# Four interleaved attention layers: side tiles in pieces of four matmuls, and an earlier first score in the full layers

## The chip, the cores and the metric

The kernel runs on one core of a Trainium2 chip. The metric is the device time of one execution in microseconds (us); the number given is a median of several runs. A profile is one execution, recorded by the hardware profiler.

## What is computed

Four layers in a row on x of 2048 positions by 512 features, 32 heads of 16: sliding attention (A), full attention (B), A, B. Each layer adds its output to x.

```python
def _A_ref(x, wqkv, wo):            # _B_ref is the same without the mask
    B, S, D = x.shape
    H = 32; Dh = D // H; W = 256
    q, k, v = ...                   # from x @ wqkv, split by heads
    scores = jnp.einsum("bhqd,bhkd->bhqk", q, k) * (Dh ** -0.5)
    idx = jnp.arange(S)
    mask = (idx[:, None] - idx[None, :] >= 0) & (idx[:, None] - idx[None, :] < W)
    scores = jnp.where(mask[None, None], scores, -1e9)
    p = _softmax(scores, axis=-1)
    o = jnp.einsum("bhqk,bhkd->bhqd", p, v)
    return o.transpose(...).reshape(B, S, D) @ wo

x = x + _A_ref(_layernorm(x), A_wqkv, A_wo)
x = x + _B_ref(_layernorm(x), B_wqkv, B_wo)
x = x + _A_ref(_layernorm(x), A_wqkv, A_wo)
x = x + _B_ref(_layernorm(x), B_wqkv, B_wo)
```

## The kernel before

**Attention.** Positions go in 4 chunks of 512 (c), heads in 8 groups of four (qd). Scores are computed transposed, keys by queries, two heads at a time in the two 64-row halves of the array, and ACT takes their exp straight from PSUM (`exps`, L718; exps are L735). In a sliding layer (0 and 2) a group has three units, each with two exps, selects on POOL that zero the masked triangles (L802, L805), and the product with the values (L812), which PE does two units later. Score matmuls are L731. A layer has 4 x 8 x 3 = 96 units. In a full layer (1 and 3) a group has 16 units, one per 128 keys; scores are L727, products with the values L779; a layer has 512 units. PSUM holds two score tiles, so the scores of a pair wait until the exp of the pair before last is done.

**The shift.** Instead of a row maximum, a bound from the squared lengths of queries and keys is subtracted. It comes in as extra rows of the score product: the queries' bound is row 3 of `qs`, the keys' is row 7 of `kf`. For it the squares of all keys are summed by heads on PE (`squares`, L535), reduced on DVE to `km` (L562), over all chunks to `kx` (L600) and made a row `mk` (L602), which goes to `kf` in DRAM (L604); then `kt`, the keys of one group, is loaded (L752). In a full layer no score can run before the last chunk of keys is in.

**Side work.** Everything else is side work, written as generators: keys, queries and values (`project`, `values`), output product with the next layer's norm (`wo`). Its matmuls are made in `mms` (L390): a tile is 12 matmuls, three terms by four blocks, of 128x128 by 512 columns, 0.222 us each by the planner's clock. In the sliding layers and the handoffs a tile is recorded at once (L402). In the full layers a matmul is cut into eight parts of 64x32 (L399), and `yield us` lets the planner put single steps between the scores; `PH["busy"]` says that a tile is open, and `Side.one` (L897) then goes on with it.

`Side` (L883) spreads the side work: after each unit of attention, `step` in a sliding layer runs work until what is spent has caught up with the work due by then:

```python
s0, due = self.spent, self.cost * self.k / (self.steps - 2)
while self.q and self.spent < due and self.spent - s0 < 3:
    c = self.one()
    if c is None or c < 0 and self.spent - s0 >= 2 and due - self.spent < 4:
        break
```

**Handoffs.** Behind a sliding layer's last unit come the works in `tails` (L1188), then the keys' shift, then `lasts` (L1190), then the full layer. `late` marks works that fill the time of the last chunk's norm. PE and SP (which issues the DMAs) run in the order of recording.

Of the kernel before, what the change touches and what calls it, by code (L numbers as in the profile page):

```python
# [19 lines left out]
P = 128  # L20
# [12 lines left out]
HEAD_START = 100  # L33
EB, XB, XNB, WB, VB, OB = 6, 4, 4, 2, 3, 5
# [155 lines left out]
def fast_path(ctx, tc, flag, a_x, a_wqkv, a_wo, b_wqkv, b_wo, out):  # L190
# [199 lines left out]
    def mms(ps, pairs, after=1.6, us=MM):  # L390


        PH["busy"] = PH["full"]
        for i, (a, b) in enumerate(pairs):
# [9 lines left out]
            if i < len(pairs) - 1:  # L404
                if PH["full"]:
                    yield us
            else:
                PH["free"] = clock[0] + (2.0 if PH["full"] else after)
                PH["busy"] = False
    TERMS = ((0, 0), (0, 1), (1, 0))  # L410
# [67 lines left out]
    def project(l, s, c, act, ht=None):  # L478
# [3 lines left out]
        w = weights(ty, s, n, *((0, D, 0) if ht is None else (ht * P, (ht + 1) * P, not act)))  # L482
# [9 lines left out]
        for t in range(NHT) if ht is None else (ht,):  # L492
# [39 lines left out]
            yield -MM if PH["full"] else -12 * MM  # L532
# [20 lines left out]
    def keys(l, c, act, ht=None):  # L553
        sqs = yield from project(l, 1, c, act, ht)

        def rest():
# [4 lines left out]
            with tc.high_priority(HEAD_START):  # L561
                nc.vector.tensor_reduce(KM[l][r, c:c + 1], ph[r], axis=AX.XY if PH["full"] else AX.X, op=ALU.max)  # L562
        pend.append((clock[0] + (4.6 if PH["full"] else 3.6), rest))
# [31 lines left out]
    def key_shift(l, ht=None):  # L595

        settle()
# [3 lines left out]
        m = vp.tile([P, QC], F16, name=f"mk{l}_{ht}", tag="m", bufs=1)  # L601
        nc.vector.tensor_scalar(m[r], ones[r], kx[r], -0.515, op0=ALU.mult, op1=ALU.mult)  # L602
        for t in range(NHT) if ht is None else (ht,):
            nc.sync.dma_start(rows(kf)[8 * t:8 * t + 8, 7, :].rearrange("h (c n) -> h c n", n=QC),  # L604
                              m[32 * t:32 * t + 8, None, :].broadcast_to([8, NQ, QC]))

    def values(l, c, act, halves=(0, 1), tiles=range(4)):
# [18 lines left out]
        for i in tiles:  # L626
# [13 lines left out]
            yield -us if PH["full"] else -12 * us  # L640

    def wo(l, c, tail):
# [4 lines left out]
        for i in range(4):  # L647
# [11 lines left out]
            yield -MM if PH["full"] else -12 * MM  # L659
# [84 lines left out]
    def load_full(l, c, qd):  # L744
        n = f"{l}_{c}_{qd}"
        pair = slice(2 * qd, 2 * qd + 2)
        qt = pp.tile([P, 2, QC], F16, name=f"qt{n}", tag="qt", bufs=2)
        nc.sync.dma_start(qt, qs[1, c][pair].rearrange("r p n -> p r n"))
        kts = []
        for v in range(2):  # L750
# [69 lines left out]
    class Work:  # L820
# [34 lines left out]
        proj = property(lambda self: self.name is not None and self.name[0] in ("K", "Q", "K3", "Q3"))  # L855
# [27 lines left out]
    class Side:  # L883
# [13 lines left out]
        def one(self, force=False):  # L897

            drain()
            if PH["full"] and PH["busy"]:  # L900
# [85 lines left out]
    def attention(l, works):  # L986
# [5 lines left out]
        for t in range(NHT if l == 3 else 1):  # L992
            for c in range(NQ):
                qds = range(2 * t, 2 * t + 2) if l == 3 else range(NQD)
                if l == 1:

                    sd = sd or Side(NT * NQD // 2, works[0], works[1], 0.33)
                    while ("Q", 1, c) not in DONE:
                        sd.one(True)
# [4 lines left out]
                for qd in qds:  # L1004
                    if (l, c, qd) == (1, 0, NQD // 2):
                        sd.finish()
                        sd = Side(NT * NQD * NQ - NT * NQD // 2, works[1], works[2], 0.33)
                    nxt = load(l, c, qd + 1) if qd + 1 in qds else None
                    a = acc[qd % 2 if win else 0]
                    began, u = clock[0], 0  # L1010
                    for f in (attn_win if win else attn_full)(l, c, qd, *ops, a):
# [15 lines left out]
                        elif u:  # L1027
                            sd.step()
# [212 lines left out]
```

## Time and profile before

| | |
|---|---|
| median of 3 runs | 2760.06 us (2759.93 to 2761.41) |
| profiled execution | 2759.5 us, of it span 2757.7 us |
| busy over the span | PE 2496.1 us (91%), ACT 2362.9 (86%), DVE 1094.9, POOL 515.8 |
| chain of work that ended last | ACT 56%, PE 23%, issue 11%, DVE 5%, DMA 3% |

Rows of the profile name an engine, a line, what is written and read, and how often; PEld is the load of weights into the array, SPq a DMA issue on SP. A wait is put down to whoever ended it. A timeline row gives start, length, and in brackets the idle time ahead and its releaser; a run of like instructions is one row (x12). The ends of matmuls are modelled.

### The profile page before, as it was taken

The numbers are of one execution on the slowest core, as the hardware profiler recorded it, in microseconds if no ns is written. First come the engines' busy times: TensorE is split into PE (matmuls) and PEld (weight loads), VectorE is DVE, ScalarE is ACT, GpSimd is POOL, SyncE is SP. The second block draws the span as 40 slices with busy tenths as digits, with TensorE's granted clock in tenths as the row PEclk, the third lists the DMA queues.
The fourth block names the chain that finished last, engine by engine and source line by source line (L and its number), as shares of the span: only waits on it lengthen the run. The fifth ranks groups of instructions, "written<-read, shape, count | busy, mean of one in ns | idle before, by whom it ended". The sixth has DMA issues, their size and how long they took to land.

```text
span 2757.7 us, 112292 instructions
## 1 busy us (share of the span) xinstructions
PE 2496.1 (91%) x50513; PEld 1100.3 (40%) x50513; DVE 1094.9 (40%) x2314; ACT 2362.9 (86%) x2683; POOL 515.8 (19%) x1074
## 2 busy tenths in 40 slices
PE   7888989999989999999998898899899999998987
PEld 3233334444433344444443333534444444433332
DVE  5564554122343335325326566323333333333333
ACT  4556654899999999999995667399999999999997
POOL 1445552001000000100105678100000000000000
PEclk9999999999999999999999999999999999999999
DMA  8888856322342224324225565623232333333332
GB/s 286 226 241 240 244 178 191 96 83 82 100 120 79 86 93 137 102 78 126 93 73 169 157 181 143 175 72 109 84 107 90 98 97 104 112 104 123 114 120 103
DMA packets 335035, 359.67 MB, mean 130 GB/s; under 512 B 113616, under 2 KB 250320, under 8 KB 328144
## 3 DMA queue, kind: packets, MB, share of 16 engines
q1 hardware_dynamic: 334544, 352.40, 42.3%
q8 instruction: 397, 6.50, 1.0%
q14 instruction: 94, 0.77, 0.1%
HBM read 239.60 MB, written 96.99 MB: 122 GB/s over the span
## 4 chain that ended last, share of the span: by engine, by line
ACT 56%; PE 23%; issue 11%; DVE 5%; DMA 3%; POOL 2%; SPq 0%; ACTq 0%; DVEq 0%; POOLq 0%
ACT e L735 55%; PE b L402 10%; PE acc L812 3%; PE acc L779 3%; PE bs L402 2%; PE s L731 2%; PE s L727 2%; PE b L399 1%; POOL e L802 1%; POOL e L805 1%; DMA qt<-qs 1%; DMA kt<-kw 0%; DMA wr<-in_A_wo_dram 0%; DVE ot L694 0%; DMA w<-wd 0%
## 5 line engine op out<-in xcount | busy, mean ns | idle before, releaser
L735 ACT ACTIVATE e<-s 128x1024 f32<-128x1024 f32 (+2 forms) x2432 | 2238.8, 1058 | 121.0 <-PE s L731 95.3
L779 PE MATMUL acc<-e,vt 64*17 64x512 f32 x16384 | 1085.0, 590 | 1.3 <-issue 1.3
L727 PE MATMUL s<-qt,kt 64*32 64x512 f16 x16384 | 849.0, 380 | 130.4 <-ACT e L735 106.6
L727 PEld LDWEIGHTS <-kt 64*32 64x32 f16 x16384 | 406.7, 89 | 944.2 <-issue 868.8
L779 PEld LDWEIGHTS acc<-e,vt 64*17 64x17 f32 x16384 | 280.5, 92 | 61.1 <-issue 1.5
L805 POOL TENSOR_SCALAR_AFFINE_SELECT e<-e 128x256 f32<-128x256 f32 x512 | 224.9, 446 | 196.5 <-ACT e L735 195.4
L802 POOL TENSOR_SCALAR_AFFINE_SELECT e<-e 128x256 f32<-128x256 f32 x448 | 198.1, 449 | 114.1 <-ACT e L735 112.3
L712 POOL TENSOR_TENSOR oh<-o,oh 128x512 f16<-128x512 f32 x31 | 36.1, 1165 | 938.1 <-DVE oh L711 884.8
L812 PE MATMUL acc<-e,vt 128*17 128x384 f32 (+2 forms) x2816 | 204.7, 396 | 5.3 <-POOL e L802 4.0
L731 PE MATMUL s<-qt,kt 64*128 64x384 f16 (+2 forms) x1408 | 129.0, 280 | 64.0 <-ACT e L735 38.2
L415 DVE TENSOR_SCALAR sa<-acc 128x512 f32<-128x512 f32 x64 | 44.3, 692 | 335.4 <-PE acc L779 335.4
L402 PE MATMUL b<-xc,w 128*128 128x512 f16 x696 | 166.1, 390 | 7.0 <-DMA w<-wd 5.8
L677 DVE SCALAR_TENSOR_TENSOR x<-b,x 128x512 f32<-128x512 f32 x122 | 83.9, 688 | 193.0 <-PE b L399 189.8
L402 PEld LDWEIGHTS <-w 128*128 128x128 f16 x816 | 77.4, 100 | 122.8 <-issue 35.8
L521 POOL TENSOR_TENSOR sq<-sp 128x512 bf16<-128x512 f16 x28 | 41.0, 1463 | 442.2 <-DVE sp L515 427.6
L506 ACT ACTIVATE sp<-b 128x512 f16<-128x512 f32 x58 | 34.7, 598 | 103.3 <-PE b L402 91.2
L731 PEld LDWEIGHTS <-kt 64*128 64x128 f16 x1408 | 54.4, 94 | 167.6 <-issue 137.0
L521 POOL TENSOR_TENSOR sq_h<-sp_h 128x512 bf16<-128x512 f16 x27 | 40.1, 1484 | 409.8 <-DVE sp_h L515 409.8
L399 PE MATMUL b<-wo,oh 64*32 64x512 f16 x2592 | 109.9, 376 | 6.2 <-DVE x L677 3.1
L399 PE MATMUL b<-xc,w 64*32 64x512 f16 x2688 | 110.9, 376 | 3.0 <-DVE j L416 2.3
L399 PE MATMUL b<-xc,w_h 64*32 64x512 f16 x2592 | 104.4, 376 | 4.1 <-DVE km L562 3.9
L415 DVE TENSOR_SCALAR j_h<-b 128x512 f32<-128x512 f32 x27 | 18.7, 691 | 218.7 <-PE b L399 187.6
(136 smaller groups left out, 1874.8 us busy)
## 6 DMA issues: line engine op xcount, KB each, us to landing
kt<-kf SPq DMA_DIRECT2D x128, 512.0 KB
qt<-qs SPq DMA_DIRECT2D x128, 256.0 KB
xd<-x SPq DMA_DIRECT2D x96, 256.0 KB
x<-xd SPq DMA_DIRECT2D x96, 256.0 KB
w<-wd SPq DMA_DIRECT2D x22, 1024.0 KB
kt<-kw SPq DMA_DIRECT2D x64, 256.0 KB
qs<-sp SPq DMA_DIRECT2D x48, 256.0 KB
wo<-wd SPq DMA_DIRECT2D x12, 1024.0 KB
```

Source lines behind the costliest of these rows:

```text
L399: nc.tensor.matmul(ps[g:g + 32, r], a[k, g:g + 32], b[k], start=(i == 0), stop=(i == len(pairs) - 1), skip_group_check=True)
L402: nc.tensor.matmul(ps, a, b, start=(i == 0), stop=(i == len(pairs) - 1))
L415: nc.vector.tensor_scalar(dst, ps[0], scale, None, op0=ALU.mult)
L521: nc.gpsimd.tensor_tensor(sq, sp[:, 0], sp[:, 0], ALU.mult)
L677: nc.vector.scalar_tensor_tensor(xs[i], p, 1 / WS, xs[i], op0=ALU.mult, op1=ALU.add)
L727: nc.tensor.matmul(ps[g:g + 32, h], kt[R * h:R * h + R, pr, kc + g:kc + g + 32], qt[R * h:R * h + R, pr], start=True, stop=True, skip_grou ...
L731: nc.tensor.matmul(ps[:, h, s0:s0 + wd_], kt[R * h:R * h + R, pr, kc:kc + P], qt[R * h:R * h + R, pr, qc:qc + wd_], start=True, stop=True)
L735: nc.scalar.activation(e[:, :, w0:w1], ps[:, :, w0:w1], AF.Exp, scale=SCALE)
L779: nc.tensor.matmul(acc[r][32 * h:32 * h + DH + 1, :], V[l, qd // 4, j // 8][k, j % 8, 4 * (qd % 4) + h, :], es_[h // 2][k, h % 2, :], star ...
L802: nc.gpsimd.affine_select(v, v, pattern=[[0, 2], [-1, P]], compare_op=ALU.is_gt, fill=0.0, base=0, channel_multiplier=1)
L805: nc.gpsimd.affine_select(v, v, pattern=[[0, 2], [1, P]], compare_op=ALU.is_ge, fill=0.0, base=0, channel_multiplier=-1)
L812: nc.tensor.matmul(a[32 * h:32 * h + DH + 1, q * P:(q + nb) * P], V[l, (4 * c + j) // 4][:, j % 4, 4 * qd + h, :], es_[h // 2][:, h % 2, s ...
```

## The change

**Pieces of four.** In a sliding layer `mms` now yields after every fourth matmul, so a tile can lie over up to three units; `PH["busy"]` is set there too, and `one` finishes the open tile before it picks other work. **First scores.** The keys of layer 1's last chunk are made in four quarters of the heads (`K1`), as layer 3's already were; only two quarters (layer 1) or one (layer 3) stand ahead of the full layer, the others are side work of it. `early_keys` and `early_queries` load the first half of the first group's keys and its queries at the end of the sliding layer; `key_shift` then writes the row for them straight into that tile in SBUF. The last chunk's values are made ahead of the full layer only for the lower heads and two of four key blocks; the rest (`last_lower`, `upper`) and layer 1's queries of chunk 1 are side work of the full layer. **Queries.** Layer 3's first queries (`Q3(0, 0)`) move from the handoff into layer 2's last chunk.

```diff
+PIECE = 4
     def mms(ps, pairs, after=1.6, us=MM):
-        PH["busy"] = PH["full"]
+        PH["busy"] = PH["full"] or PH["win"]
...
                 if PH["full"]:
                     yield us
+                elif PH["win"] and i % PIECE == PIECE - 1:
+                    yield PIECE * us
...
+    def last(us):
+        return -(1 if PH["full"] else PIECE if PH["win"] else 12) * us
...
-            yield -MM if PH["full"] else -12 * MM
+            yield last(MM)
...
-    def keys(l, c, act, ht=None):
+    def keys(l, c, act, ht=None, then=None):
...
                 nc.vector.tensor_reduce(KM[l][r, c:c + 1], ph[r], axis=AX.XY if PH["full"] else AX.X, op=ALU.max)
+                if then is not None:
+                    then(l, ht)
...
-    def key_shift(l, ht=None):
-        settle()
+    def key_shift(l, ht):
...
+        if ht == 0:
+            for pr in range(2):
+                nc.sync.dma_start(PRE["k"][7:P:R, pr, :].rearrange("r (c n) -> r c n", n=QC),
+                                  m[2 * pr:2 * pr + 2, None, :].broadcast_to([2, 2, QC]))
+        nc.sync.dma_start(rows(kf)[8 * ht:8 * ht + 8, 7, :].rearrange("h (c n) -> h c n", n=QC),
+                          m[32 * ht:32 * ht + 8, None, :].broadcast_to([8, NQ, QC]))
+        DONE["S", l, ht] = clock[0]
+    PRE = {}
+    def early_keys(l):
+        PRE["k"] = pp.tile([P, 2, S // 2], F16, name=f"kt{l}_0_0_0", tag="kt", bufs=3)
+        nc.sync.dma_start(PRE["k"], kf[0:2, :, :S // 2].rearrange("r p n -> p r n"))
+    def early_queries(l):
+        PRE["q"] = pp.tile([P, 2, QC], F16, name=f"qt{l}_0_0", tag="qt", bufs=2)
+        nc.sync.dma_start(PRE["q"], qs[1, 0][0:2].rearrange("r p n -> p r n"))
...
     def one(self, force=False):
-            if PH["full"] and PH["busy"]:
+            if PH["busy"]:
                 return self.piece(PH["last"])
...
+                    while (l, c, qd % 2) == (1, 0, 1) and qd + 1 in qds and ("S", 1, (qd + 1) // 2) not in DONE:
+                        if ("K1", (qd + 1) // 2) in DONE and not PH["busy"]:
+                            settle()
+                        else:
+                            sd.one(True)
...
+                        while not win and (c, qd, u) == (0, 0, NT - 5) and ("V", l, 3, (0,), 2) not in DONE:
+                            sd.one(True)
...
+    def K1(ht, act=False):
+        return Work(later(keys, 1, NQ - 1, act, ht, key_shift), PK / 4, ("K1", ht), [("T", 1, NQ - 1), ("P", 1, 1)], True)
...
-        return [OO(2, 2), T(3, 2), K3(2, 0, True)]
+        return [OO(2, 2), T(3, 2), Q3(0, 0, True), K3(2, 0, True)]
...
+    def last_lower(l):
+        return VV(l, 3, False, (0,), (), range(2, 4))
...
-        a += [Q(1, c, False) for c in (2, 3)]
+        a += [Q(1, c, False) for c in (1, 2, 3)]
...
-        a = [Q3(c + 1, t)] if c < 3 else []
+        a = [last_lower(3)] if (t, c) == (0, 0) else []
+        a += [Q3(c + 1, t)] if c < 3 else []
...
-    works = [[side0(c) for c in range(NQ)], [[upper(1, c) for c in range(3)], side1()], [side2(c) for c in range(NQ)],
+    works = [[side0(c) for c in range(NQ)], [[last_lower(1), K1(2), upper(1, 2), upper(1, 3), K1(3)], side1()], [side2(c) for c in range(NQ)],
...
-    tails = {0: [VV(1, 2, True, (0,)), OO(0, 3, True), VV(1, 1, True, (0,), late(1)), Q(1, 1, True, late(1)), T(1, 3), K(1, 3)],
-             2: [VV(3, 0, True, (0,)), OO(2, 3, True), VV(3, 1, True, (0,), late(3)), VV(3, 2, True, (0,), late(3)), Q3(0, 0, True, late(3)), T(3, 3), K3(3, 0, True)]}
-    lasts = {0: [VV(1, 3)], 2: [VV(3, 3, True, (0,)), VV(3, 0, True, (1,))]}
+    tails = {0: [VV(1, 2, True, (0,)), OO(0, 3, True), VV(1, 1, True, (0, 1), late(1)), VV(1, 0, True, (1,), late(1)), T(1, 3), K1(0, True), K1(1, True)],
+             2: [VV(3, 0, True, (0,)), OO(2, 3, True), VV(3, 1, True, (0,), late(3)), VV(3, 2, True, (0,), late(3)), VV(3, 0, True, (1,), late(3)), T(3, 3), K3(3, 0, True)]}
+    lasts = {l: [VV(l + 1, 3, True, (0,), (), range(2))] for l in (0, 2)}
...
             attention(l, works[l] + [tails[l]])
+            settle()
+            early_keys(l + 1)
+            early_queries(l + 1)
             all_of(tails[l], lasts[l])
-            key_shift(l + 1, 0 if l else None)
             all_of(lasts[l], works[l + 1][0])
+            settle()
```

The order of the instructions shows it at three places. First PE in layer 2, chunk 1, between the groups qd 1 and qd 2 (`s_` are scores, `acc` the products with the values, `oh` and `wo` the operands of an output tile). Before, PE goes from the products of one unit straight to the next scores:

```order
L812 MATMUL acc_82<-e_1_1_0_0_29748,vt_0_0_0_15544 17x128 x2
L812 MATMUL acc_82<-e_1_1_0_1_29758,vt_0_0_0_15544 17x128 x2
L812 MATMUL acc_82<-e_1_1_0_0_29748,vt_1_0_0_21586 17x384 x2
L812 MATMUL acc_82<-e_1_1_0_1_29758,vt_1_0_0_21586 17x384 x2
L731 LDWEIGHTS kt_1_2_29738
L731 MATMUL s_1_2_0_0_29858<-qt_1_2_29739,kt_1_2_29738 128x128
```

In the change four matmuls of an output tile stand there; these are the last of them and the scores behind:

```order
L403 LDWEIGHTS oh_0_5_29808
L403 MATMUL b_30186<-wo_0_30049,oh_0_5_29808 128x512
L760 LDWEIGHTS kt_1_2_30103
L760 MATMUL s_1_2_0_0_30228<-qt_1_2_30104,kt_1_2_30103 128x128
L760 LDWEIGHTS kt_1_2_30103
```

and the same tile (b_30186) goes on behind the products of the next unit:

```order
L842 MATMUL acc_82<-e_1_1_1_0_30145,vt_1_0_0_22380 17x256 x2
L842 MATMUL acc_82<-e_1_1_1_1_30154,vt_1_0_0_22380 17x256 x2
L403 LDWEIGHTS oh_0_5_29808
L403 MATMUL b_30186<-wo_0_30049,oh_0_5_29808 128x512
L403 LDWEIGHTS oh_0_7_30046
L403 MATMUL b_30186<-wo_0_30049,oh_0_7_30046 128x512
```

So the tile was cut after its eighth matmul, and a unit that had no side work has four matmuls of it. Second, PE ahead of layer 1, behind the last key tile (`sq` the squares of a quarter of the heads, `wv` the value weights). Before, the square sums of all four quarters are followed by four value tiles of 512 columns, then by the first scores:

```order
L546 MATMUL b_5637<-sq_1_3_2_5613,hsum 32x512
L546 LDWEIGHTS hsum
L546 MATMUL b_5637<-sq_1_3_3_5633,hsum 32x512
L402 LDWEIGHTS xc_3_5384
L402 MATMUL bs_5655<-wv_3_0_0_5544,xc_3_5384 128x512
```

In the change the first quarter's square sum follows two key tiles, and a value tile has 256 columns:

```order
L403 LDWEIGHTS w_1_3_h_5530
L403 MATMUL b_5554<-xc_3_5388,w_1_3_h_5530 128x512
L553 LDWEIGHTS hsum
L553 MATMUL bs_5567<-sq_1_3_h_0_5548,hsum 32x512
L403 LDWEIGHTS xc_3_5388
L403 MATMUL b_5586<-wv_3_0_0_5552,xc_3_5388 128x256
```

Two such value tiles, with the second quarter's square sum between them, remain ahead of the first scores. Third, SP at the same place, before:

```order
L526 DMA kf<-sp_1_3_3_5630 128x2x512
L527 DMA kf<-sp_1_3_3_5630 128x512
L604 DMA kf<-mk_None 8x4x512 x4
L752 DMA kt_0_0_0_5724<-kf 128x2x1024
L752 DMA kt_0_0_1_5726<-kf 128x2x1024
```

and in the change, where kt's first half (kt_0_0_0) was loaded long before and only its row comes now, behind a weight load and the key writes:

```order
L371 DMA wv_3_0_2_5584<-wd_2_111 128x8x256
L533 DMA kf<-sp_1_3_h_1_5577 128x2x512
L534 DMA kf<-sp_1_3_h_1_5577 128x512
L616 DMA kt_0_0_0_5232<-mk_0_5572 2x2x512 x2
L618 DMA kf<-mk_0_5572 8x4x512
```

The write of mk to DRAM and the load of kt behind it no longer stand between the last keys and the first scores; a small copy within SBUF does.

36 lines of the change are left out of this document (20 added, 16 removed).

## The prediction

> **What bounds the kernel now.** First the page's slices: which engine is full, and where.
>
> ```profile
> PE   7888989999989999999998898899899999998987
> ACT  4556654899999999999995667399999999999997
> ```
>
> Each digit is a 69 us slice. ACT stands at 9 in two long stretches, the full layers 1 and 3, and at 4 to 6 in the sliding layers, where PE is at 8 or 9 but not full. I cut the span at these borders. The columns are the stretch and its length, then the busy time of PE, weight loads, DVE, ACT and POOL with their counts, PE's granted clock, DMA's busy share, GB/s.
>
> ```profile
> 54.00:437.00 383.00, 339.37 (x2950) 135.34 (x2949) 201.62 (x476) 233.31 (x308) 195.23 (x483) 0.94 0.79 226
> 437.00:495.00 58.00, 55.71 (x328) 28.65 (x328) 24.37 (x55) 17.60 (x35) 1.96 (x6) 1.00 0.69 207
> 495.00:1446.00 951.00, 887.39 (x22560) 400.61 (x22552) 320.24 (x640) 943.32 (x1026) 59.46 (x46) 1.00 0.31 94
> 1446.00:1732.00 286.00, 253.86 (x2574) 99.06 (x2562) 175.22 (x406) 190.57 (x228) 198.91 (x483) 0.99 0.55 160
> 1732.00:1783.00 51.00, 45.31 (x327) 30.85 (x319) 20.58 (x49) 12.61 (x28) 0.00 (x0) 0.97 0.72 204
> 1783.00:2740.00 957.00, 871.34 (x21614) 386.24 (x21622) 307.86 (x577) 943.97 (x1024) 57.52 (x42) 1.00 0.33 103
> ```
>
> In order: sliding layer 0, a handoff, full layer 1, sliding layer 2, a handoff, full layer 3. In a full layer ACT works 943 us of 951 and of 957: its exps set the time, and a full layer can only start earlier or lose. The handoffs are PE work in a row with ACT nearly idle. In the sliding layers nothing is full, so I ask what PE waits for in layer 2 and in layer 0 (us in total, times, longest).
>
> ```profile
> PE s L731 <- ACT e L735: 23.5, 43, 1.1
> ...
> PEld acc L812 <- POOL e L802: 9.0, 26, 1.2
> ```
> ```profile
> PEld L731 <- DMA kt<-kw: 15.0, 3, 7.9
> PE s L731 <- ACT e L735: 14.8, 22, 1.6
> ```
>
> Layer 2 loses 23.5 + 9.0 = 32.5 us in many small waits for exps and selects, which an even spread of the side work can remove. Layer 0 loses 15.0 in three long waits for kt, with DMA 0.79 busy, and only 14.8 in small ones for ACT.
>
> **Part 1, pieces of four.** PE's timeline in layer 2:
>
> ```profile
> 1611.83 0.61 PE L731 MATMUL s<-qt,kt 64*128 64x384 f16 x8
> 1612.37 1.06 PE L812 MATMUL acc<-e,vt 128*17 128x128 f32 x16
> 1613.36 2.76 PE L402 MATMUL b<-wo,oh 128*128 128x512 f16 x12
> 1616.06 0.61 PE L731 MATMUL s<-qt,kt 64*128 64x128 f16 x8
> 1616.60 1.06 PE L812 MATMUL acc<-e,vt 128*17 128x256 f32 x16
> 1617.64 0.40 PE L731 MATMUL s<-qt,kt 64*128 64x256 f16 x4
> 1618.56 0.39 PE L731 MATMUL s<-qt,kt 64*128 64x256 f16 x4 [0.52 <-ACT e L735]
> ```
>
> A unit with a tile takes 4.23 us (1611.83 to 1616.06), a plain one 1.58 (1616.06 to 1617.64), and behind a plain one the next scores wait 0.52 for ACT. ACT was idle beside the tile and is late beside the plain unit. Counted along PE's order, layer 2 has before its last unit 62 plain units, 32 with a tile and one with two; the change has 26 plain, 41 with four matmuls, 20 with eight, 5 with twelve, 3 with sixteen. If waits go with the plain units, 32.5 us become 32.5 x 26/62 = 13.6, a gain of 19. Against it: one tile more (the last layer's first queries, 12 matmuls, 2.6 us), and 69 - 33 = 36 more units in which PE enters side work. An entry costs 0.11 us, as the chain of waits shows: a tile behind attention takes 2.70, one behind another tile 2.59.
>
> ```profile
> 447.04 2.59 PE b L402 x12
> ```
> ```profile
> 1609.20 2.70 PE b L402 x12
> ```
>
> That is 4 us, so 19 - 2.6 - 4 = 12 gained. A unit with four matmuls would take 1.58 + 4 x 2.59/12 + 0.11 = 2.55; ACT's work is 190.57/96 = 2.0 per unit and POOL's 198.91/96 = 2.1, so it should not wait, but only 0.5 us covers it, and selects come in lumps. I take **-10** for layer 2, near the 12 that the counts give, between -26 (all waits go) and +6.6 (none goes).
>
> [...]
>
> In layer 0 the side work is the same 792 matmuls of 512 columns; plain units go from 30 to 18. Of 14.8 us of ACT waits 14.8 x 12/30 = 6 could go, 1 returns as entries, and where DMA is the limit the rest turns into longer waits for kt. In the order nearly all side jobs end at the same unit or one later, so K and Q are not written sooner. I take **-3**, between -12 and +8.
>
> **Part 2, first handoff.** PE's timeline before, from the moment the last chunk's normalized x lands:
>
> ```profile
> 471.79 2.75 PE L402 MATMUL bs<-xc,w 128*128 128x512 f16 x12 [1.14 <-DMA xc<-xh]
> 474.47 0.40 PE L546 MATMUL b<-sq,hsum 128*32 128x512 bf16 x4
> ...
> 484.40 2.76 PE L402 MATMUL bs<-wv,xc 128*128 128x512 f16 x12
> ...
> 494.86 0.62 PE L727 MATMUL s<-qt,kt 64*32 64x512 f16 x16
> ```
>
> Behind 471.8 stand four key tiles and four value tiles to 494.86. The change leaves two key tiles and two half value tiles there. Ahead of 471.8 the work is equal (a query chunk of four tiles out, four tiles of values in), so I keep that start: xc lands by DMA, not by PE. Two key tiles end at 477.1. The first one's square sum follows at once, then km, kx, mk on DVE:
>
> ```profile
> 484.50 0.69 DVE L562 TENSOR_REDUCE km<-b 128x1 f32<-128x512 f32 x1 [0.40 <-PE b L546]
> ...
> 485.50 0.35 DVE L602 TENSOR_SCALAR mk_None<-ones,kx_None 128x512 f16<-128x512 f16 x1
> ```
>
> From 484.50 to 485.85 is 1.35 us; with the square sum's 0.4 ahead of it mk stands at about 478.9. On SP the two writes of the second key tile are ahead of its copies into kt. The second handoff has rows for both steps: its key tile ends at 1770.0 (Part 3) and its second write goes out at 1771.90 and is issued by 1772.35, 2.4 us behind; and a small copy of mk at 1774.93 lets the load that waits for it go at 1777.53, 2.6 us later.
>
> ```profile
> 1771.90 0.45 SPq L527 DMA_DIRECT2D kf<-sp_h  x1
> ...
> 1774.93 0.32 SPq L604 DMA_DIRECT2D kf<-mk  x1
> ...
> 1777.53 1.41 SPq L752 DMA_DIRECT2D kt<-kf  x3
> ```
>
> So the copies go at 477.1 + 2.4 = 479.5 and 479.8, and the first scores run near 482.4. The half value tiles must not come later: their weights can go only when the first key tile is done, at 474.4, and take less than a load twice their size, so they land by 479.6, and 2 x 1.3 us more are 482.2.
>
> ```profile
> 454.84 5.22 DMA w<-wd
> ```
>
> I take **-12.5** (494.86 to 482.4), between -16 (the scores follow the key tiles' own work) and -6 (half).
>
> **Part 3, second handoff.**
>
> ```profile
> 1758.69 2.76 PE L402 MATMUL bs<-xc,w_h 128*128 128x512 f16 x12 [0.19 <-DMA w_h<-wd]
> ...
> 1765.56 4.45 PE L402 MATMUL bs<-xc,w_h 128*128 128x512 f16 x12 [3.79 <-DMA x<-xd]
> ...
> 1771.35 0.38 PE L546 MATMUL bs<-sq_h,hsum 128*32 128x512 bf16 x1 [1.03 <-ACT sq_h L519]
> ...
> 1783.07 0.63 PE L727 MATMUL s<-qt,kt 64*32 64x512 f16 x16 [0.75 <-DMA kt<-kf]
> ```
>
> The query tile at 1758.69 moves into layer 2, half of the value tiles from behind the key tile come ahead of it and cover most of the wait to 1765.56. The key tile then takes 2.7 instead of 4.45 if the clock holds: in the trace it ran at 0.50 just there.
>
> ```profile
> 1766.20:1769.60 3.40, 3.40 (x9) 1.21 (x8) 0.00 (x0) 0.00 (x0) 0.00 (x0) 0.50 0.64 211
> ```
>
> From its end at 1768.2: 1.4 to the square sum (1770.0 to 1771.35), 0.4 for it, 1.35 on DVE, 0.3 for the first copy, 2.6 for the second to land: first scores near 1774.3, **-9**, between -11 and -4. [...]
>
> **Part 4, full layers.** Layer 1 takes 50 matmuls of 512 columns more while it runs and 10 behind its last scores. At 2.59/12 = 0.216 each (a whole matmul's time, which its eight parts share here), the 10 are 2.2 us; the 50 are 11 us of PE under 951 - 887 = 64 us of slack, but in the later chunks they raise the densest stretches, and PE has little room in those:
>
> ```profile
> 1350.00:1400.00 50.00, 48.46 (x1240) 22.29 (x1225) 17.62 (x34) 49.88 (x55) 5.61 (x4) 1.00 0.28 90
> ```
>
> I take **+5**, from +2 to +13. Layer 3 takes 12 more: **+0.5**, from 0 to 3. What is late next behind the early scores is kt's second half, read back from DRAM behind the row's write: 2.6 us for the write and 1783.07 - 1777.53 = 5.5 for the load, 8 us, while the first half feeds 8 units of 951/512 = 1.86, 15 us.
>
> **Sum.** -3 - 12.5 + 5 - 10 - 9 + 0.5 = -29 against the profiled execution's 2759.5 us (span 2757.7 and 1.8 around it) gives 2730.5. The median of the three runs is 2760.06, 0.6 more: **2731**.
>
> **Rivals.** (a) *Pieces give nothing*: PE's waits move to exps and to kt, entries stay. Layer 2 +6.6, layer 0 +1: -12.5 - 9 + 5 + 0.5 + 7.6 = -8.4, 2751.7. For it: ACT and POOL work 2.0 and 2.1 us per unit, so units of 2.55 us run three engines near their limit. Against: ACT's idle beside every tile is plain in the rows. (b) *Handoffs give half*, since SP, in order, holds the row copies behind a weight load and the key writes, or x lands later: -11 for -21.5, 2741. (c) *Pieces give all*: layer 2 -26, layer 0 -12: 2706. (d) *Slower*: the tiles end later in pieces, so the K and Q writes come later, and the chunks' first loads, which wait for them, stall PE. In layer 0 one such wait was 7.9 us. If each of the six later chunk starts of layers 0 and 2 had one such wait more, that is 6 x 7.9 = 47 us: 2778. It decides once a chunk's queries end within a landing of its start; in the order they end 10 units or more ahead, and that speaks against it. (e) *It does not do what it says*: the early loads wait for their buffers, scores start as before; then only Part 1 and the smaller PE work remain, near (b).
>
> **Chances.** Forecast 0.62 (2718 to 2740), (b) with (e) 0.13, (a) 0.13, (c) 0.07, (d) 0.05. The range 2715 to 2750 leaves out (d), (c) and the upper half of (a). A change of 0.2%, 5.5 us, is about what a measurement of this kernel can tell from none. Faster by more: 0.62 + 0.13 + 0.07 + most of (a) = 0.91; within: 0.04; slower: 0.05.
>
> **What would show it.** Right: layer 2's PE waits for ACT near 10 instead of 23.5 us, four-matmul units near 2.55 us; first full scores 12.5 and 9 us sooner after the sliding layers' ends; the second handoff's key tile at full clock; ACT still over 0.98 in the full layers. Wrong: plain 0.5 us waits now in the units with four matmuls (a), a long wait for mk or wv ahead of the first scores (b), long kt waits at chunk starts (d), ACT below 935 of 951 us in layer 1 (Part 4).

## The result, and the profile after

The changed kernel takes **2725.1 us** (median of four runs, 2721.88 to 2731.55) beside 2760.4 us for the kernel before, measured with it (four runs, 2759.93 to 2761.41): the ratio is 0.9876, with a 95% interval of 0.9862 to 0.9890. It is faster by 35 us, six more than forecast and inside the range. The profiled execution took 2721.88 us, 2720.2 of it span.

The stages below are cut at PE's rows: a sliding layer from its first score to the end of its last product with the values, a handoff from there to the first full score, a full layer from its first score to the next layer's first (layer 3: to the end of its last score). In line numbers of the changed kernel, L760 are the sliding scores, L764 the exps, L842 the products, L756 the full scores, L403 a side tile, L553 a square sum, L832 and L835 the selects.

| us | layer 0 | handoff 1 | layer 1 | layer 2 | handoff 2 | layer 3 |
|---|---|---|---|---|---|---|
| before | 385.6 | 55.8 | 953.2 | 284.2 | 50.8 | 953.6 |
| after | 374.4 | 45.6 | 954.4 | 274.8 | 42.6 | 953.5 |
| moved | -11.2 | -10.2 | +1.2 | -9.4 | -8.2 | -0.1 |
| forecast | -3 | -12.5 | +5 | -10 | -9 | +0.5 |

Each cell is one profile, and the moves add to 37.9 us, as the profiled execution is the fastest of the four. In the other profiles below, layer 0 with pieces took 372.0 to 377.7 us, layer 1 of the change 952.7 to 955.2 and layer 2 of the change 274.1 to 276.6, so that a move of one or two us in a cell says nothing.

First the slices of the page, in tenths of a slice's time:

```profile
PE   7888999999998999999998999899999999988997
ACT  4575664999999999999995777499999999999996
```

The picture is that of before: ACT is full in the full layers, and PE is near full but not full in the sliding ones. What moved is idle time of PE, some of its busy time in layer 0, and the PE work of the handoffs. The windows of the two sliding layers and the two handoffs (length, then busy time of PE, weight loads, DVE, ACT, POOL, then PE's granted clock, DMA share, GB/s), of before for the sliding layers:

```profile
53.49:439.04 385.55, 341.85 (x2968) 136.15 (x2969) 201.88 (x476) 233.31 (x308) 196.86 (x487) 0.94 0.79 226
1448.06:1732.25 284.19, 252.05 (x2551) 98.74 (x2547) 175.22 (x406) 189.55 (x226) 198.91 (x483) 0.99 0.55 160
```

and of the changed kernel:

```profile
53.67:428.04 374.37, 337.60 (x2969) 133.46 (x2969) 201.90 (x476) 237.05 (x308) 197.66 (x487) 0.96 0.81 234
1428.04:1702.80 274.76, 251.99 (x2569) 95.49 (x2561) 175.23 (x408) 193.39 (x228) 201.12 (x483) 0.98 0.62 175
428.04:473.68 45.64, 41.84 (x244) 23.93 (x242) 20.40 (x50) 11.73 (x26) 0.32 (x1) 0.96 0.55 156
1702.80:1745.47 42.67, 37.65 (x279) 26.60 (x278) 19.19 (x47) 10.59 (x24) 0.00 (x0) 1.00 0.70 189
```

In layer 2 PE's busy time is the same (252.05 and 251.99), though a tile came in: the whole gain is idle time, 284.19 - 252.05 = 32.1 us before and 22.8 after. In layer 0 the idle time fell from 43.7 to 36.8 us, and PE's busy time by 4.3 us at a clock of 0.96 instead of 0.94.

What PE and the weight load (PEld) waited for in layer 2 of the changed kernel (us in total, times, longest):

```profile
PE s L760 <- ACT e L764: 11.8, 20, 1.1
PE s L760 <- DMA qt<-qs: 7.4, 3, 3.6
...
PEld acc L842 <- POOL e L832: 9.9, 34, 1.3
```

The waits for exps are half of the 23.5 us of before. Before, all of them stood behind a unit without side work; now 10.7 of the 11.8 us do. The weight load's waits for selects, 9.0 us before, did not fall. But the weight load waited while PE still worked on earlier matmuls: PE's own waits for selects, 0.5 and 0.2 us in two rows before and 0.6 now, were small from the start. The first of these rows:

```profile
PE acc L812 <- POOL e L802: 0.5, 1, 0.5
```

Layer 0 of the changed kernel:

```profile
PE s L760 <- ACT e L764: 8.6, 14, 1.9
PE b L403 <- DVE km L569: 5.5, 1, 5.5
```
```profile
PEld L760 <- DMA kt<-kw: 10.4, 3, 8.7
```

Here too the waits for ACT fell (14.8 before), but so did those for kt (15.0 before). The one for km grew from 1.2 us.

PE's timeline of the first handoff, from the last values ahead of the new key tiles to the first score:

```profile
457.94 1.47 PE L403 MATMUL b<-wv,xc 128*128 128x256 f16 x12
460.49 2.76 PE L403 MATMUL bs<-xc,w_h 128*128 128x512 f16 x12 [1.08 <-DMA w_h<-wd]
463.09 2.75 PE L403 MATMUL b<-xc,w_h 128*128 128x512 f16 x12
465.77 0.39 PE L553 MATMUL bs<-sq_h,hsum 128*32 128x512 bf16 x1
468.41 1.81 PE L403 MATMUL b<-wv,xc 128*128 128x256 f16 x12 [2.24 <-DMA wv<-wd]
470.14 0.61 PE L553 MATMUL bs<-sq_h,hsum 128*32 128x512 bf16 x1
470.69 2.52 PE L403 MATMUL b<-wv,xc 128*128 128x256 f16 x12
473.68 0.41 PE L756 MATMUL s<-qt,kt 64*32 64x512 f16 x8 [0.48 <-DMA kt<-mk]
```

and DVE at the same time:

```profile
466.20 0.68 DVE L569 TENSOR_REDUCE km<-bs 32x1 f32<-32x512 f32 x1 [1.59 <-PE bs L553]
...
467.40 0.13 DVE L608 TENSOR_REDUCE kx<-km 32x1 f32<-32x4 f32 x1
470.79 0.68 DVE L569 TENSOR_REDUCE km<-bs 32x1 f32<-32x512 f32 x1 [3.25 <-PE bs L553]
471.50 0.34 DVE L613 TENSOR_SCALAR mk<-ones,kx 32x512 f16<-32x512 f16 x1
```

The first quarter's bound kx is there at 467.53, but its row mk is made at 471.50: in DVE's order the second quarter's km stands between, and that waits for a square sum on PE which stands behind a value half tile, which waits 2.24 us for its weights. The second handoff has no such knot; its key tile ran at full clock (1.00 over 1737.46:1740.22), as forecast:

```profile
1737.46 2.76 PE L403 MATMUL b<-xc,w_h 128*128 128x512 f16 x12 [1.33 <-DMA w_h<-wd]
...
1745.47 0.63 PE L756 MATMUL s<-qt,kt 64*32 64x512 f16 x16 [2.02 <-DMA kt<-mk]
```

### The profile page after: what moved, and what is told of

It is laid out like the page before. It is cut to its first block, busy times and chain, and to the rows that moved or that the text cites. A ratio compares the mean times of both kernels' runs of the same rounds, so it can differ in the third digit from the quotient of the medians.

```text
span 2720.2 us, 113346 instructions
## 1 busy us (share of the span) xinstructions
PE 2487.6 (91%) x51023; PEld 1095.7 (40%) x51023; DVE 1110.8 (41%) x2342; ACT 2363.1 (87%) x2671; POOL 526.7 (19%) x1080
## 3 DMA queue, kind: packets, MB, share of 16 engines
q1 hardware_dynamic: 340664, 353.46, 43.7%
## 4 chain that ended last, share of the span: by engine, by line
ACT 55%; PE 23%; issue 11%; DVE 7%; DMA 3%; POOL 1%; SPq 0%; ACTq 0%; DVEq 0%; POOLq 0%
ACT e L764 55%; PE b L403 9%; PE acc L842 4%; PE s L760 2%; PE acc L809 2%; PE s L756 2%; PE bs L403 1%; PE b L400 1%; DVE xh L455 1%; DVE xh L449 1%; DMA kt<-kw 1%; DVE xn L449 0%; DVE ot L723 0%; DMA wr<-in_A_wo_dram 0%; DMA wv<-wd 0%
## 5 line engine op out<-in xcount | busy, mean ns | idle before, releaser
L764 ACT ACTIVATE e<-s 128x1024 f32<-128x1024 f32 (+2 forms) x2432 | 2240.7, 1056 | 149.9 <-PE s L760 101.0
L756 PE MATMUL s<-qt,kt 64*32 64x512 f16 x16384 | 850.8, 381 | 121.4 <-ACT e L764 99.8
L756 PEld LDWEIGHTS <-kt 64*32 64x32 f16 x16384 | 407.0, 89 | 931.3 <-issue 852.0
L835 POOL TENSOR_SCALAR_AFFINE_SELECT e<-e 128x256 f32<-128x256 f32 x512 | 224.9, 445 | 189.7 <-ACT e L764 188.5
L832 POOL TENSOR_SCALAR_AFFINE_SELECT e<-e 128x256 f32<-128x256 f32 x448 | 199.2, 450 | 94.4 <-ACT e L764 91.9
L842 PE MATMUL acc<-e,vt 128*17 128x384 f32 (+2 forms) x2816 | 201.8, 394 | 6.4 <-POOL e L832 6.2
L403 PE MATMUL b<-xc,w 128*128 128x512 f16 x660 | 161.7, 392 | 9.8 <-DVE km L569 5.5
L760 PE MATMUL s<-qt,kt 64*128 64x384 f16 (+2 forms) x1408 | 121.3, 279 | 43.7 <-ACT e L764 20.4
L400 PE MATMUL b<-xc,w 64*32 64x512 f16 x3072 | 126.5, 376 | 2.7 <-DVE j L423 1.5
L400 PE MATMUL b<-xc,w_h 64*32 64x512 f16 x2784 | 111.0, 376 | 3.9 <-DVE km L569 3.9
L403 PEld LDWEIGHTS <-w 128*128 128x128 f16 x720 | 67.0, 100 | 116.3 <-issue 46.4
L422 DVE TENSOR_SCALAR vt<-b 128x256 f32<-128x256 f32 (+1 forms) x36 | 18.4, 512 | 232.9 <-PE b L400 232.9
L760 PEld LDWEIGHTS <-kt 64*128 64x128 f16 x1408 | 52.0, 95 | 140.9 <-issue 114.8
```

Source lines behind the costliest of these rows:

```text
L400: nc.tensor.matmul(ps[g:g + 32, r], a[k, g:g + 32], b[k], start=(i == 0), stop=(i == len(pairs) - 1), skip_group_check=True)
L403: nc.tensor.matmul(ps, a, b, start=(i == 0), stop=(i == len(pairs) - 1))
L422: nc.vector.tensor_scalar(dst, ps[0], scale, None, op0=ALU.mult)
L756: nc.tensor.matmul(ps[g:g + 32, h], kt[R * h:R * h + R, pr, kc + g:kc + g + 32], qt[R * h:R * h + R, pr], start=True, stop=True, skip_grou ...
L760: nc.tensor.matmul(ps[:, h, s0:s0 + wd_], kt[R * h:R * h + R, pr, kc:kc + P], qt[R * h:R * h + R, pr, qc:qc + wd_], start=True, stop=True)
L764: nc.scalar.activation(e[:, :, w0:w1], ps[:, :, w0:w1], AF.Exp, scale=SCALE)
```

## The experiments

The theory: pieces of four take idle time from PE in both sliding layers, about 20 us; shorter handoffs give about 18; full layers take moved work for nothing. The rivals: layer 0's gain is where its loads happen to fall; an entry into side work costs what the pieces give; the first scores are held by something other than what the change shortened. Times are medians; the kernel before stood at 2758.0 to 2759.7 us beside these runs.

**Whole tiles in the changed kernel.**

```diff
-PIECE = 4
+PIECE = 12
```

> The changed kernel with its tiles whole again in the sliding layers (a piece is 12 matmuls); the handoffs and the full layers stay as changed. Theory A, the pieces take PE's waits for ACT and POOL in layer 2 and a mix of waits in layer 0: both losses come back, layer 0 goes from 374.4 to 385.5 us, layer 2 from 274.8 to 284.2 + 2.6 (the tile that moved in) = 286.8, and the time is 2725 + 11.1 + 12 = 2748 us, with PE's waits for exps in layer 2 again near 23 us. Rival B, layer 0's 11 us come from where its loads happen to fall and not from the pieces: layer 0 stays within 3 us of 374, layer 2 loses 12, 2737 us. Rival C, the pieces give only the waits that the plain units lost on paper and the rest is the handoffs' doing: under 2735 us.

Measured: 2744.28 us (0.9938 of before, 0.9925 to 0.9951). Both layers go back, layer 0 to 389.3 us and layer 2 to 283.9, and the handoffs stay at 44.7 and 42.1. Two waits of its layer 0 and one of its layer 2:

```profile
PE s L760 <- ACT e L764: 14.8, 22, 1.6
...
PEld L760 <- DMA kt<-kw: 18.0, 4, 9.1
```
```profile
PE s L760 <- ACT e L764: 25.1, 45, 1.1
```

They are back at those of before (14.8, 15.0 and 23.5 us) or over them, kt's included. So layer 0's gain is the pieces', and rivals B and C fall.

**The pieces alone, in the kernel before** (the edits to `mms`, `one` and the yields as in the change):

```diff
-        PH["busy"] = PH["full"]
+        PH["busy"] = PH["full"] or PH["win"]
...
+                elif PH["win"] and i % PIECE == PIECE - 1:
+                    yield PIECE * us
```

> The kernel before with the pieces of four alone. Theory A: layer 0 gains 11 us, layer 2 12 us (9.4 and the 2.6 of the tile that does not move in here), nothing else moves: 2760.4 - 23 = 2737 us, with layer 2 near 272 us and the handoffs still 56 and 51 us. Rival B (layer 0's gain is not the pieces'): 2748 us with layer 0 near 385. If the parts of the change do not add up (the sum of this gain and of that of the handoffs alone is not the whole), one of them feeds the other: then this run and the run with whole tiles together miss 35 us by over 5.

Measured: 2747.54 us (2741.39 to 2752.86; 0.9949, 0.9935 to 0.9963). Layer 0 376.0 and layer 2 277.4, so both gain; but the time is 12 us under before where 23 were expected. Together with the 15.4 us of the run with whole tiles that is 27.5 of 35. That misses by over 5, the mark set for parts that feed each other; the next run looks for the tie. By stages, layer 2 waited 4.9 us for kt (1.6 in the changed kernel), and handoff 2 and layer 1 were 1.8 and 2.6 us longer than before.

**The pieces and layer 3's first queries, in the kernel before.**

```diff
-        return [OO(2, 2), T(3, 2), K3(2, 0, True)]
+        return [OO(2, 2), T(3, 2), Q3(0, 0, True), K3(2, 0, True)]
...
```

> The kernel before with the pieces of four and with layer 3's first queries moved into layer 2's last chunk; nothing else of the handoffs is changed. Theory O, this move is what ties the two parts of the change together (it fills plain units of layer 2, 26 instead of 29, and takes a tile of 2.7 us out of the second handoff): the pieces give their 20 us here, layer 2 takes 275 us and the second handoff 48, 2736 to 2740 us. Rival P, it ties nothing and the 12 us of the pieces alone lie low by the spread of that kernel's runs: 2.7 us off that kernel's time of 2747.5, 2743 to 2747 us, with layer 2 at 277 us or more.

Measured: 2742.61 us (2741.12 to 2748.89; 0.9944, 0.9930 to 0.9957): by the time 0.4 us under rival P's range, by the stages theory O, with layer 2 at 275.9 and the second handoff at 46.6. What is missing lies in the full layers, 956.0 and 956.0 us instead of 953.2 and 953.6. Why they were longer there I cannot say; so it stays open why the two parts of the change give 27.5 us in all by themselves and 35 together. The intervals of the three ratios, 3.6 to 3.9 us either way, could make up most of that. In its second handoff the wait and the slow tile of before stand as they were, with nothing put ahead of the key tile in the queries' place:

```profile
1746.47 4.44 PE L403 MATMUL bs<-xc,w_h 128*128 128x512 f16 x12 [3.69 <-DMA xc<-xh]
```

**Pieces in layer 0 alone, and the changed kernel again beside it.**

```diff
+        PH["cut"] = l == 0
...
-                elif PH["win"] and i % PIECE == PIECE - 1:
+                elif PH["cut"] and i % PIECE == PIECE - 1:
```

> The changed kernel with pieces of four in layer 0 alone; layer 2 has whole tiles. Theory A, the pieces act in each layer by themselves: layer 0 stays near 374 us with 37 to 41 us of PE idle, layer 2 goes back to 284 us with 23 to 25 us of waits for exps, and the time is 2725 + 9 = 2734 us. Rival B (layer 0's gain is not the pieces'): both layers as with whole tiles, 2744 us. As the two parts of the change gave 27.5 us alone and 35 together, a time under 2731 would say that layer 0's pieces are worth more beside the new handoffs.

> The changed kernel itself once more, beside these. If the 6 us between it and the kernel of the two further handoff edits are real, it takes 2722 to 2728 us here; if they were the spread of the runs, 2717 to 2721.

Measured: 2730.19 us (2727.3 to 2732.62) and 2722.58 us (2721.15 to 2724.52) on the same chip. The windows of layers 0 and 2, first with pieces in layer 0 alone:

```profile
54.79:432.52 377.73, 341.02 (x2969) 134.19 (x2970) 201.69 (x476) 237.11 (x308) 197.64 (x487) 0.95 0.80 232
1430.79:1713.55 282.76, 250.60 (x2569) 99.78 (x2562) 175.98 (x409) 190.38 (x228) 197.50 (x483) 1.00 0.60 174
```

and in the changed kernel:

```profile
53.14:425.22 372.08, 336.54 (x2969) 133.26 (x2970) 201.95 (x476) 237.02 (x308) 197.61 (x487) 0.96 0.80 235
1424.46:1701.04 276.58, 252.23 (x2569) 95.69 (x2562) 176.02 (x408) 193.39 (x228) 201.44 (x483) 0.98 0.61 174
```

PE's idle time in layer 0, with pieces in both runs, is 36.7 and 35.5 us; in layer 2 it is 32.2 us with whole tiles and 24.4 with pieces. So each layer's pieces act in that layer; layer 2's are worth 7.6 us here, and layer 0's the other 12 to 14 of the way to the run with whole tiles (12 by the two ratios, 14 by the medians, which are from different chips). The time under 2731 us was to say that layer 0's pieces are worth more beside the new handoffs. Layer 0 itself, 377.7 us here and 376.0 with the pieces alone, does not bear that out.

Both layer 2 windows hold the same matmuls. Whole tiles run at clock 1.00 and PE is busy 250.60 us; with pieces and twice the entries (69 units with side work instead of 35) it is busy 252.23 at 0.98. By these two clocks about 0.02 x 252.23 = 5 of the 252.23 us are the clock's (an estimate). The entries cost nothing that shows.

**Pieces of two.**

```diff
-PIECE = 4
+PIECE = 2
```

> The changed kernel with pieces of two. In layer 2 the units with side work go from 66 to 74, those without from 29 to 21. Theory A: PE's waits for exps in layer 2 go on falling with the plain units, 11.8 x 21/29 = 8.5, and an entry costs 0.05 us or less: layer 2 between 270 and 274 us, layer 0 within 3 us of 374, 2720 to 2725 us. Rival D, an entry costs 0.11 us and more as two matmuls do not cover it: the 8 entries and the finer cuts cost what the waits give back, 2725 to 2730 us.

Measured: 2729.58 us (2722.09 to 2733.45), layer 0 376.3, layer 2 279.5. In its layer 2:

```profile
PE s L760 <- ACT e L764: 8.3, 15, 1.0
PE b L403 <- DMA xc<-xh: 7.3, 1, 7.3
PE s L760 <- DMA kt<-kw: 6.0, 1, 6.0
```

The 66 and 29 units of the expectation are those of the pieces alone; the changed kernel has 69 and 26, so its count of plain units gives 11.8 x 21/26 = 9.5 us of waits for exps. They fell to 8.3, somewhat under that. What takes the gain back is neither theory's: waits of 7.3 us for a normalized x and 6.0 for kt, which the changed kernel has not or not as long (1.6 for kt). That jobs end later in smaller pieces would explain them; it was not followed up. The medians leave open whether the kernel as a whole is slower (0.9870 to 0.9898 of before, against 0.9862 to 0.9890).

**Weights of the handoffs in a spare ring of buffers.** The key tiles ahead of the full layers take their weights in the buffers of the sliding layers' values, which are free by then.

```diff
-        w = weights(ty, s, n, *((0, D, 0) if ht is None else (ht * P, (ht + 1) * P, l == 3 and not act)))
+        w = weights(ty, s, n, *((0, D, 0) if ht is None else (ht * P, (ht + 1) * P, l == 3 and not act or then is not None and act)))
...
```

> The changed kernel with the last key tiles' weights of both handoffs in the ring of buffers that the sliding layers' values have just left, so that they and the last values' weights are sent sooner. This moves the first quarter's row mk ahead of the second quarter's km on DVE as well. Theory E, the first scores are held by PE's waits for weights (1.08 + 2.24 us in the first handoff, 1.68 + 1.33 in the second) and by the half clock behind them: the first handoff goes from 45.6 to 42 to 43.5 us, the second from 42.7 to 40 to 41.5, 2719 to 2722 us. Rival F, the normalized x that lands sets the start of the last key tiles: they begin no sooner, and only the value half tiles move, 1 us in all.

Measured: 2725.51 us (2720.34 to 2727.91), handoff 1 40.5 us, handoff 2 42.2. PE in the first handoff:

```profile
458.83 1.47 PE L403 MATMUL b<-wv,xc 128*128 128x256 f16 x12
460.14 2.75 PE L403 MATMUL bs<-xc,w_h 128*128 128x512 f16 x12
...
469.46 0.41 PE L756 MATMUL s<-qt,kt 64*32 64x512 f16 x8 [0.61 <-DMA kt<-mk]
```

The key tile follows the values without a wait, so the normalized x did not hold it: theory E for the first handoff, 5.1 us of stage (3.8 against the changed kernel's second profile, 44.3). That is more than expected; mk no longer stood behind km as well, and the run does not part the two. In the second handoff nothing came; there its wait of 1.7 us was for other weights (next run). The total did not follow: layer 1 was 956.3 instead of 954.4. The three later kernels with this ring have 956.6 to 958.3 us there, and six profiles of the changed layer 1 without it 952.7 to 955.2. So layer 1 gives back 2 to 3 us of the earlier start, for a reason that no run here shows.

**Two more edits in the second handoff**: the upper values' weights in the spare ring too, and the key tile's square sum one half tile sooner.

```diff
-        pend.append((clock[0] + (4.6 if PH["full"] else 3.6), rest))
+        pend.append((clock[0] + (4.6 if PH["full"] else 3.6 if PH["win"] else 1.2), rest))
...
-VV(3, 0, True, (1,), late(3)), T(3, 3)
+VV(3, 0, True, (1,), late(3), ring=1), T(3, 3)
```

> The kernel with the spare ring, with two more edits in the second handoff: the last upper values' weights use that ring too, and the last key tile's square sum goes behind one value half tile instead of two. Theory E: the wait of 1.73 us for those weights goes and mk is made 1.3 us sooner, so that the second handoff goes from 42.2 to 39 to 40.5 us, and the first stays at 40.5; 2720 to 2723 us. Rival F: the key tile now waits for the normalized x, so that only the 1.3 us come.

Measured: 2719.15 us (2716.23 to 2719.29; 0.9858 of before, 0.9841 to 0.9874), handoffs 41.5 and 39.7 us: theory E for the second handoff, while the first took 1 us more and layer 1 958.3. The changed kernel measured again, 2722.58 us, falls just into the 2722 to 2728 that were to make the difference real, but the intervals of the two ratios (0.9854 to 0.9887 for the changed kernel) overlap, so it is not shown by the time.

**The row by way of DRAM** (no early load of the first keys).

```diff
-        if ht == 0:
+        if ht == 0 and "k" in PRE:
...
-            early_keys(l + 1)
             early_queries(l + 1)
```

> The changed kernel without the early load of the first keys: the row mk goes to DRAM alone, and the first half of the keys is loaded behind it, as before; the short run of PE work ahead of the full layers stays. Theory G, the direct copy into the loaded tile is what lets the scores start: the first scores wait for a write of 2.6 us and a load of 5.5 us behind mk instead of one small copy, so the first handoff goes from 45.6 to 50 to 52 us and the second from 42.7 to 47 to 49, 2735 to 2739 us. Rival H, the shorter PE work is what counts, as PE still has value tiles to do behind mk: under 3 us in all, 2728 us.

Measured: 2737.85 us (2735.16 to 2740.47), handoffs 51.0 and 50.2: 5.4 and 7.6 us lost, theory G. Its first scores, in the two handoffs:

```profile
479.16 1.05 PE L756 MATMUL s<-qt,kt 64*32 64x512 f16 x16 [5.79 <-DMA kt<-kf]
```
```profile
1761.11 1.05 PE L756 MATMUL s<-qt,kt 64*32 64x512 f16 x16 [6.58 <-DMA kt<-kf]
```

**Fewer matmuls in layer 1.**

```diff
-            yield from mms(ps, [(w[:, k, a, w0:w0 + P], xc[:, b, k, :]) for a, b in TERMS for k in range(NC)], 2.2)
+            yield from mms(ps, [(w[:, k, a, w0:w0 + P], xc[:, b, k, :]) for a, b in TERMS[:1 if (l, s) == (1, 0) and PH["full"] else 3] for k in range(NC)], 2.2)
```

> The changed kernel with one of three terms in the queries that layer 1 makes for itself (chunks 1 to 3), which leaves the low-order parts of the product out: 96 matmuls of 512 columns fewer in layer 1, the 10 behind its last scores among them. Theory I, ACT's exps set a full layer's time and what PE does inside is free: only the 10 matmuls come off, 2 us, and from the first score to the last nothing moves by over 1.5 us. Rival J, each matmul inside costs what the prediction's 5 us for 60 says, 0.08 us: 8 us.

Measured: 2723.09 us (2722.05 to 2724.41). Layer 1 takes 951.4 us, 3.0 less than in the changed kernel: 1.55 of it behind the last exp (1.04 instead of 2.59 us to layer 2's first score), 1.4 within. Other profiles of the changed layer 1 differ by up to 2.5 us, so the 1.4 cannot be told from nothing; 0.08 us for each of the 86 matmuls inside would be 7 and is excluded. Theory I.

**Layer 0's weight loads behind the keys.** In chunk 0 PE waits 8.2 us for the keys of group 4 (6.85 in the kernel of the two further handoff edits, to which this edit was made); their load stands on SP behind eight loads of an output weight.

```diff
+        if (ty, s) == (0, 3):
+            yield wait(3)
         raw = load_w(ty, s)
```

> The kernel of the two further handoff edits, with layer 0's eight small loads of an output weight (in chunk 0) sent behind the load of the keys of group 4 and not ahead of it. Theory K, PE's wait of 8.2 us for these keys in layer 0 comes from the place in SP's queue: their load goes out 9 us sooner, the wait falls under 2 us, and layer 0 takes 367 to 370 us instead of 374 to 376; 2713 to 2717 us. Rival L, the wait passes to what the weight loads now push back (the writes of the next chunk's queries and the transposes, and the loads of the next groups): layer 0 gains under 2 us.

Measured: 2724.57 us (2722.81 to 2727.67) beside 2719.15 without the edit, layer 0 375.4 us instead of 372.0. PE at the place:

```profile
99.04 0.50 PE L762 MATMUL s<-qt,kt 64*128 64x384 f16 x4 [1.44 <-DMA kt<-kw]
...
110.86 0.50 PE L762 MATMUL s<-qt,kt 64*128 64x384 f16 x4 [3.18 <-DMA kt<-kw]
```

The wait is down to 1.44 us there and comes back at the next group; nothing is gained: rival L. The kernel lost 5.4 us; by the profiles layer 0 took 3.4 us more and layer 3 took 3.0 more, the latter for a reason that is not shown.

**Pieces of three, with the handoff edits.**

```diff
-PIECE = 4
+PIECE = 3
```

> The kernel of the two further handoff edits with pieces of three. Units without side work go from 29 to 22 in layer 2, as with pieces of two, but a tile lies over fewer units. Theory M, PE's waits for ACT in layer 2 fall with the plain units to 11.8 x 22/29 = 9 us and the tiles end in time: 2714 to 2718 us. Rival N, the tiles end later, as with pieces of two, where PE waited 7.3 us for a normalized x and 6 us for keys in layer 2: 2719 to 2724 us.

Measured: 2717.65 us (2716.27 to 2721.45; 0.9853, 0.9837 to 0.9870), layer 2 277.1 us with 7.5 us of waits for exps. Between M and N: the waits fell under the 11.8 x 22/26 = 10.0 us of the count of plain units, and a wait of 4.7 us for kt came. It is the fastest kernel of the study, 4.9 us under the changed kernel measured beside it, though the intervals of the two ratios (0.9854 to 0.9887 for the changed one) overlap; against pieces of four with the same handoffs nothing can be told.

## Why the prediction was right, and where its steps failed

The time was right to 6 us. The mechanisms of layer 2 and of the handoffs were right, and their three terms came within 2.3 us each; that the total came so near is in part luck. Layer 0 and the full layers missed by 12.6 us one way and the other three terms by 3.7 the other way, 8.9 us in the profile, of which the median of four shows six. And inside layer 2's term two errors nearly cancelled.

**Layer 2, -10 forecast, -9.4 found.** The wait that carried the term behaved as said: 23.5 us became 11.8 ("near 10"), 8.3 with pieces of two, and 25.1 with whole tiles, which is 0.38 to 0.45 us for each plain unit. Two other steps failed. "Layer 2 loses 23.5 + 9.0 = 32.5 us" adds waits of the weight load for selects to waits of PE. PE's own rows have 0.7 us for selects, so the 9.0 x 36/62 = 5.2 us that were to come from them were not there to win, and the weight load's waits did not fall either (9.9). Against that, the 4 us for 36 more entries and the 2.6 us for one tile more do not show in PE's busy time. A plain unit without a wait over 0.15 us took 1.65 us (median), one with four matmuls 2.50 (median of 41; 2.55 was forecast, with 0.11 for the entry), one with eight 3.36, one with twelve before the change 4.23. Each step is the time of four matmuls, 4 x 2.59/12 = 0.86 us, and leaves nothing for an entry. The 2.70 beside 2.59 of one chain was no price of an entry. And longer waits for queries (7.4 us in three where 4.6 stood in two) and for kt (1.6 us) took some of the gain.

**Layer 0, -3 forecast, -11.2 found: the mis-sized term.** The 6 us of waits for exps came off as counted (14.8 to 8.6). The step that failed is "where DMA is the limit the rest turns into longer waits for kt". They became shorter, 15.0 to 10.4 us, and 18.0 with whole tiles says that this is the pieces' doing. One wait of 7.4 us, for the keys of chunk 1's group 4, went (with whole tiles it was 7.3):

```profile
196.47 1.03 PE L731 MATMUL s<-qt,kt 64*128 64x128 f16 x8 [7.41 <-DMA kt<-kw]
```

SP's rows before show what stood ahead of that load:

```profile
179.00 4.96 SPq L470 DMA_TRANSPOSE xc<-xh  x2
...
186.15 1.10 SPq L761 DMA_DIRECT2D qt<-qs  x1
187.30 1.28 SPq L762 DMA_DIRECT2D kt<-kw  x1
```

and in the changed kernel:

```profile
171.34 8.36 SPq L477 DMA_TRANSPOSE xc<-xh  x3
...
181.88 0.43 SPq L791 DMA_DIRECT2D qt<-qs  x1
182.35 0.50 SPq L792 DMA_DIRECT2D kt<-kw  x1
```

The transposes and writes ahead of the load are through 5 us sooner, and the scores that need it start at 188.0 without a wait instead of 196.5. Meanwhile PE's waits for km and for selects grew by 4.3 and 2.1 us, so that its idle time fell by 6.9 in all. The forecast put nothing for the clock, and there lies the rest: 4.3 us of PE's busy time went with the granted clock's rise from 0.94 to 0.96. The idle part is the surer one. In the twelve profiles with pieces in layer 0 PE was idle for 34.6 to 37.0 us, with whole tiles for 43.7 and 46.5; the clock over the layer was 0.95 and 0.96 in the three windows with pieces above, 0.94 before and 0.93 with whole tiles. I had looked whether jobs end sooner by units, and not what else stands in SP's queue ahead of a load.

**First handoff, -12.5 forecast, -10.2 found.** Three of its steps failed. "I keep that start: xc lands by DMA" was right in number only: the key tile began 32.4 us behind layer 0's end, 32.7 forecast, but held by its own weights; with those sent sooner it began at 31.1 without a wait. Then mk was to stand 1.35 us behind the square sum; DVE's order put the second quarter's km between, so that the row left 4 us late. And the value weights, forecast to land in time, came 2.24 us late, and PE's clock fell behind that wait:

```profile
469.40:472.80 3.40, 3.40 (x17) 1.87 (x15) 1.51 (x4) 0.38 (x1) 0.00 (x0) 0.50 0.47 157
```

With the spare ring this handoff took 40.5 us, 15.3 under before: the mechanism had more in it than I forecast.

**Second handoff, -9 forecast, -8.2 found.** Its steps held: values ahead of the key tile, the tile at 2.76 instead of 4.45 us, the direct copy (worth 7.6 us by itself). That the clock would hold was an estimate; behind a wait of 1.33 us the tile ran at 1.00. The counterpart is the run with pieces and queries alone: with a wait of 3.69 us the tile took 4.44.

**Full layers, +5 and +0.5 forecast, +1.2 and -0.1 found.** The 10 matmuls behind the last scores cost 1.55 us (2.2 forecast). The 50 inside cost nothing that shows, where I had put 3 us for the dense stretches; ACT was busy for 944.8 of 951.7 us in layer 1, as forecast.

**The rivals.** Pieces that give nothing, (a), are excluded by both layers' returns with whole tiles; handoffs that give half, (b), by -18.4 of -21.5. Pieces that give all, (c), came near in layer 0 (-11.2 where it had -12) and not in layer 2. Longer waits at chunk starts, (d), did not come: the longest for queries in layer 2 is 3.6 us, 3.8 before, and the one for kt in layer 0's chunk 1 went. That the early loads would wait for their buffers, (e), did not happen: scores ran 2.2 and 2.5 us behind the start of mk's row (473.68 - 471.50; 1745.47 - 1742.96 on DVE).

## What to carry to other kernels

Where an engine's small waits stand in the stretches without side work, count those stretches in the old and the new order: here the wait per stretch held, at 0.34 to 0.45 us, from 62 down to 21 of them. Check that the waits counted are the engine's own, and not those of a weight load beside which it works. Look in the order in which SP issues the DMAs for what stands ahead of each load that ends a wait, since a change of pace on PE moves that too. Ahead of a stage with a fixed length, trace each row of its start through every engine's order, as one wait (here for weights) can pass from PE to DVE and to the copy behind it.

## What the runs showed of the hardware

PE's granted clock was read at four waits of the handoffs. In the kernel before, the second handoff's key tile waited 3.79 us: PE was busy for 0.64 of the 3.40 us from 1762.80, and 1766.20:1769.60 ran at 0.50. In the changed kernel's first handoff a value half tile waited 2.24 us: PE was busy for 1.16 of the 3.40 us from 466.00, and 469.40:472.80 ran at 0.50. The changed kernel's second key tile, behind a wait of 1.33 us, ran at 1.00. With the pieces and queries alone in the kernel before, the second key tile waited 3.69 us and took 4.44, and the clock over 1745:1751 was 0.72. How long a wait the clock takes without falling is not shown.

The time of one kernel differed with its clock: of six runs of the pieces alone the fastest took 2741.39 us at a mean clock of 0.989, the slowest 2752.86 at 0.985. Which of the two led the other is not shown.
